# Attention and a max-out layer on one core: the linear layers on seven blocks of 512 tokens instead of eight of 448

## The chip, the core and the metric

The kernel runs on one core of one Trainium2 chip. A core has a matrix engine (TensorE, PE in the profile; its weight loads, LDWEIGHTS, stand in a row of their own, PEld), a vector engine (VectorE, DVE), a scalar engine (ScalarE, ACT), a general engine (GpSimd, POOL) and SyncE (SP), whose queue issues the DMA transfers here. Operands lie in on-chip memory (SBUF) of 128 partitions; matmuls write to PSUM banks of 512 float32 a partition. The metric is device time of one execution in microseconds.

## The reference, cut to what matters

```python
# q, k, v: (8, 12, 448, 64) float32
scores = scale * np.matmul(q, k.transpose(0, 1, 3, 2)) - np.log(S)      # S = 448, scale = 1/8
attn = 1.0 / (1.0 + np.exp(-scores))
attn_out = np.matmul(attn, v)
# x: 3584 tokens of 768 features; w1, w2, w3, w_out: 768 x 768
x = attn_out.transpose(0, 2, 1, 3).reshape(B * S, H * D)
h = np.maximum(np.maximum(x @ w1, x @ w2), x @ w3)
return (h @ w_out).astype(np.float32)
```

## The kernel before

**Attention.** 24 rounds, one for each group of four heads of a batch element. A round loads the next round's q and k (two tiles `qk`) and v through SyncE's queue (`load`), computes scores by TensorE (`scores`, `last_scores`, L330 and L342), their sigmoid on ScalarE (L312), and the weighted sums of v (`weigh`, `last_weigh`, L350 and L359). VectorE splits q/k into a high and a low part of the reduced-precision type float32r (`qk_split`, L321 and L322), so that three cheap products stand for one float32 product. `finish` copies a round's result from PSUM (L378) and stores it to the DRAM tensors `x_dram` (L379), features by tokens, in two halves of 384 features. Beside it each round decodes one piece of the weights (`decode`, L165 to L204), and GpSimd makes sums of weight blocks (`w_combine`, L141).

**Linear layers.** Two layers: three matrices w1, w2, w3 with the maximum over them, then w_out. Each matrix is cut in halves both ways, and a *pair* of token blocks makes the other factor two by two, so that seven products of sums of blocks stand for eight (`PRODUCTS`: name of the weight sum, name of the token sum, PSUM bank). A *visit* is one of four stages (three blocks of output features of layer one, then layer two) for one pair; it runs three outputs q, each with seven products of nine matmuls (three float32r terms for three slices of 128 features, `product`, L451). With 448 tokens a block there are four pairs and 16 visits.

**Token operands.** A pair's four blocks are loaded whole (`x_block`, L218), four differences made by GpSimd (`x_combine`, L229), then each of seven operands is split: `x_hi` on ScalarE (L260), `x_lo` on VectorE (L264), into tiles of their own (`xhi_*`, `xlo_*`). For the first pair the loads and differences run inside attention, rounds 9 to 20. The differences of layer one are stored to `t_dram` once (`t_store`, L242), and stages 1 and 2 load all seven operands from there and `x_dram` (`x_load_all`).

**What sets the order.** Every instruction is pinned to the order of the program text on its engine; SyncE's queue is in that order too, and a DMA whose data is not ready holds all behind it. In the linear layers, tables keyed by (visit, output, product) say after which product a split (`his`, `los`), a weight split (`ws`), a weight load (`w_loads`) or a decode is issued. `put` takes a product from PSUM (L521 to L529) and, at the end, stores it to `h_dram` or `outT` (L537).

Of the kernel before, what the change touches and what calls it, by code (L numbers as in the profile page):

```python
# [17 lines left out]
P = 128  # L18
D = 64

LEAST = 1.125 * 2.0**-15

# [12 lines left out]
    ("s4", "b22", 2),  # L35
)
# [3 lines left out]
def attention_then_maxout(  # L40
# [8 lines left out]

# [43 lines left out]
    t_dram = [dram.tile([P, 4, HALF, S], F32, name=f"t_dram{p}") for p in range(B // 2)]  # L93
# [6 lines left out]
    xs_p = pool(ctx, "xs", 1)  # L100
    m_p = pool(ctx, "m", 1)
    xo_p = [pool(ctx, "xo", 1)]
    ps_av = pool(ctx, "ps_av", 1, space=PSUM)


# [18 lines left out]
    def w_stage():  # L124
        return {name: ws_p.tile([P, HP], F32, name=f"ws_{name}") for name in BLOCKS}

# [6 lines left out]
        "s3": ("a11", "a21", ALU.subtract),  # L133
# [22 lines left out]
    def decoding(dec_p, todo, bufs, ahead, square_p):  # L156
# [11 lines left out]
        def decode(raw, out):  # L168
# [3 lines left out]
            square = square_p.tile([P, S], F32, name="c")[:, :HP]  # L172
# [35 lines left out]
    SUMS = {"t1": ("b12", "b11"), "t2": ("b22", "t1"), "t3": ("b22", "b12"), "t4": ("b21", "t2")}  # L208
    TOKENS = tuple(SUMS)

    def x_block(r, src, p, row, th, k=None):

        name = f"b{row + 1}{th + 1}"
        if name not in r:
            r[name] = xs_p.tile([P, HALF, S], F32, name=f"xs_{name}")
        ks = slice(0, HALF) if k is None else slice(k, k + 1)
        t = (2 * p + th) * S
        pin(nc.sync.dma_start(out=r[name][:, ks], in_=src[row][:, ks, t : t + S]))  # L218

    def x_combine(r, names=TOKENS, ks=range(HALF)):  # L220

        for name in names:
            if name not in r:
                r[name] = (
                    r["b12"] if name == "t3" else xs_p.tile([P, HALF, S], F32, name=f"xs_{name}")
                )
            in0, in1 = SUMS[name]
            for k in ks:
                pin(nc.gpsimd.tensor_tensor(  # L229
                    out=r[name][:, k], in0=r[in0][:, k], in1=r[in1][:, k], op=ALU.subtract  # L230
                ))

    def x_load(src, p):
        r = {}
        for row, th in ((0, 0), (0, 1), (1, 1), (1, 0)):
            x_block(r, src, p, row, th)
        x_combine(r)
        return r

    def t_store(r, p):  # L240
        for k, name in enumerate(TOKENS):
            pin(nc.sync.dma_start(out=t_dram[p][:, k], in_=r[name]))  # L242

    def x_load_all(p):
        r = {}
        for _, name, _ in PRODUCTS:
            if name in TOKENS:
                tile_name = "xs_b12" if name == "t3" else f"xs_{name}"
                r[name] = xs_p.tile([P, HALF, S], F32, name=tile_name)
                pin(nc.sync.dma_start(out=r[name], in_=t_dram[p][:, TOKENS.index(name)]))  # L250
            else:
                x_block(r, x_dram, p, int(name[1]) - 1, int(name[2]) - 1)
        return r

    FIRST = [x for _, x, _ in PRODUCTS[:1]]

    def x_hi(name, r):
        hi = xo_p[name not in FIRST].tile([P, HALF, S], F32R, name=f"xhi_{name}")
        lo = xo_p[name not in FIRST].tile([P, HALF, S], F32R, name=f"xlo_{name}")
        pin(nc.scalar.copy(out=hi, in_=r[name]))  # L260
        return name, r[name], hi, lo

    def x_lo(name, x, hi, lo):
        pin(nc.vector.tensor_tensor(out=lo, in0=x, in1=hi.bitcast(F32), op=ALU.subtract))  # L264
        x_ops[name] = hi, lo


    def attention(stack):


# [102 lines left out]
        def finish(n, pss, pool=m_p, names=("m11", "m12")):  # L373
            b, f = fours[n]
            for g, ps in enumerate(pss):
                k = 2 * f + g
                o = pool.tile([P, S], F32, name=names[g])
                pin(nc.vector.tensor_copy(out=o, in_=ps[:, :S]))  # L378
                pin(nc.sync.dma_start(  # L379
                    out=x_dram[k // HALF][:, k % HALF, b * S : (b + 1) * S], in_=o  # L380
                ))

# [9 lines left out]
        before, xs = None, {}  # L392
        terms = [(loads[0][0][0],) * 2]
        for n in range(len(fours) + 1):
# [10 lines left out]
            else:  # L405
                for name in FIRST:
                    x_lo(*x_hi(name, xs))
            if before:
# [6 lines left out]
                finish(n - 1, pss)  # L415
            last = last_scores(ts)
# [5 lines left out]
            part = n - 9  # L422
            if 0 <= part < 4 * HALF:
                k, block = divmod(part, 4)
                row, th = ((0, 1), (0, 0), (1, 1), (1, 0))[block]
                x_block(xs, x_dram, 0, row, th, k)
                x_combine(xs, ((), ("t1",), ("t2", "t3"), ("t4",))[block], (k,))
            if n == len(fours) - 1:
                t_store(xs, 0)
# [5 lines left out]
        return xs, lambda *to: finish(len(fours) - 1, pss, *to)  # L435

    with ExitStack() as stack:
        xs, finish = attention(stack)


    xo_p.append(pool(ctx, "xo2", 1, reuse_waits="tile"))
# [4 lines left out]
    def product(ps, w, x, first):  # L446
# [3 lines left out]
        for n, (wt, xt, k) in enumerate(terms):  # L450
            pin(nc.tensor.matmul(  # L451
                ps[:, :S], wt[:, k * P : (k + 1) * P], xt[:, k],
# [3 lines left out]


    pairs = list(range(B // 2))
    visits = [(st, p) for st in range(STAGES) for p in (pairs[::-1] if st == 1 else pairs)]
    done, LAST = len(visits), STAGES - 1  # L460

    his, los, ws, w_loads = {}, {}, {}, {}

    for n in range(1, done):
# [16 lines left out]
        if (st == LAST, p) != (st0 == LAST, p0):  # L483
            for k, (_, name, _) in enumerate(PRODUCTS):
                his[n - 1, 2, k] = name
            keys = [(n - 1, 2, k) for k in range(1, 5)] + [(n, 0, k) for k in (0, 2, 3)]
            for key, (_, name, _) in zip(keys, PRODUCTS):
                los[key] = name
    w_next, split = {}, {}

    decodes = [
        (n, *at)
        for n in range(len(pairs) - 1, 3 * len(pairs) - 1)
        for at in ((0, 6), (1, 3), (1, 6))
    ]
# [4 lines left out]
    x_first = xs  # L500
    for _, name, _ in PRODUCTS[1:4]:
        x_lo(*x_hi(name, xs))
    next(background)
    for k in (1, 2, 3):
        his[0, 0, k - 1] = los[0, 0, k] = PRODUCTS[k + 3][1]

    for n, (st, p) in enumerate(visits):
        nst, np_ = visits[n + 1] if (n, 2, 0) in his else (None, None)
        if nst in (1, 2):
            xs = x_load_all(np_)  # L510
        m = {}
        for q in range(3):
            ps, p1, u2, u3 = {}, None, None, None

            def put(name, y, add):

                y = y[:, :S]
                if st == LAST or q == 0:
                    m[name] = m_p.tile([P, S], F32, name=f"m{name}")
# [6 lines left out]
                else:  # L526
                    c = c_p.tile([P, S], F32, name="c")
                    pin(nc.vector.tensor_tensor(out=c, in0=y, in1=add, op=ALU.add))
                    pin(nc.vector.tensor_tensor(out=m[name], in0=c, in1=m[name], op=ALU.max))  # L529
                if st == LAST or q == 2:  # L530
                    half, t = int(name[0]) - 1, (2 * p + int(name[1]) - 1) * S
                    if st == LAST:
                        row = (q + 3 * half) * P
                        dst = outT[row : row + P, t : t + S]
                    else:
                        dst = h_dram[half][:, st, t : t + S]
                    pin(nc.sync.dma_start(out=dst, in_=m[name]))  # L537

            for k, (wname, xname, bank) in enumerate(PRODUCTS):
                here = n, q, k  # L540
                first = k < 4 or bank == 1
                if first:
                    ps[bank] = ps_y.tile(
                        [P, 512], F32, name=f"ps_y{bank}", bufs=2 if bank < 2 else 1
                    )
# [77 lines left out]
```

## Time and profile before

| | |
|---|---|
| time, median of 3 runs (lowest, highest) | 884.38 us (882.63, 886.62) |
| span of the profiled execution | 882.5 us |
| TensorE busy | 874.1 us (99%) |
| weight loads (PEld) | 696.1 us (79%) |
| VectorE | 621.3 us (70%) |
| ScalarE | 392.9 us (45%) |
| GpSimd | 183.2 us (21%) |
| moved by DMA | 161.87 MB, mean 183 GB/s |

A single run's time and the profiled execution's span are two measures: the span goes from the first to the last instruction of one execution, and that execution's own time is not among the three. Ends of matmuls are modelled in the profile, so a busy TensorE is not one at its peak; the starts are measured, and the step from one start to the next is what a matmul costs in a full stream.

### The profile page before, as it was taken

The numbers are of one execution on the slowest core, as the hardware profiler recorded it, in microseconds if no ns is written. First come the engines' busy times: TensorE is split into PE (matmuls) and PEld (weight loads), VectorE is DVE, ScalarE is ACT, GpSimd is POOL, SyncE is SP. The second block draws the span as 40 slices with busy tenths as digits, with TensorE's granted clock in tenths as the row PEclk, the third lists the DMA queues.
The fourth block names the chain that finished last, engine by engine and source line by source line (L and its number), as shares of the span: only waits on it lengthen the run. The fifth ranks groups of instructions, "written<-read, shape, count | busy, mean of one in ns | idle before, by whom it ended". The sixth has DMA issues, their size and how long they took to land. (4 is left out here: it accounts for less than half of the span.)

```text
span 882.5 us, 12993 instructions
## 1 busy us (share of the span) xinstructions
PE 874.1 (99%) x4866; PEld 696.1 (79%) x4866; DVE 621.3 (70%) x875; ACT 392.9 (45%) x499; POOL 183.2 (21%) x148
## 2 busy tenths in 40 slices
PE   8999999999999999999999999999999999999998
PEld 4544455444459999999999999999999998899997
DVE  3677568766866948678696888878778596736442
ACT  5777767776672413342353343235334253423320
POOL 0100022023102563502100020210001543760600
PEclk9999999999999999999999999999999999999999
DMA  6667666786647455414745642484563426162412
GB/s 225 208 227 240 226 236 224 243 279 228 214 158 275 174 217 165 174 50 141 292 159 207 241 147 70 148 298 170 182 263 114 150 77 222 65 209 94 169 72 83
DMA packets 74350, 161.87 MB, mean 183 GB/s; under 512 B 6960, under 2 KB 53808, under 8 KB 74288
## 3 DMA queue, kind: packets, MB, share of 16 engines
q1 hardware_dynamic: 74208, 160.82, 52.0%
q8 instruction: 38, 0.62, 0.3%
q10 hardware_dynamic: 80, 0.23, 0.1%
q14 instruction: 24, 0.20, 0.1%
HBM read 109.90 MB, written 51.12 MB: 182 GB/s over the span
## 5 line engine op out<-in xcount | busy, mean ns | idle before, releaser
L312 ACT ACTIVATE a<-ps_s,bias_s 128x896 f32<-128x896 f32 x168 | 156.4, 1007 | 78.6 <-PE ps_s L342 59.4
L451 PE MATMUL ps_y<-xhi_t,wlo_s 128*128 128x448 f32 x432 | 158.1, 366 | 0.1
L451 PE MATMUL ps_y<-xhi_t,whi_s 128*128 128x448 f32 x432 | 158.0, 366 | 0.0
L451 PE MATMUL ps_y<-xlo_t,whi_s 128*128 128x448 f32 x432 | 157.9, 366 | 0.0
L350 PE MATMUL ps_av<-a,v 128*64 128x448 f32 x576 | 118.6, 548 | 0.0
L451 PE MATMUL ps_y<-xhi_b,wlo_a 128*128 128x448 f32 x288 | 105.4, 366 | 0.0
L451 PE MATMUL ps_y<-xlo_b,whi_a 128*128 128x448 f32 x288 | 105.3, 366 | 0.0
L451 PE MATMUL ps_y<-xhi_b,whi_a 128*128 128x448 f32 x288 | 105.3, 366 | 0.0
L141 POOL TENSOR_TENSOR ws_s<-ws_a,ws_a 128x384 f32<-128x384 f32 x12 | 14.3, 1194 | 412.9 <-DMA ws_a<-w_dram 315.8
L549 ACT COPY p<-ps_y 128x448 f32<-128x448 f32 x48 | 25.5, 531 | 156.4 <-PE ps_y L451 156.4
L451 PEld LDWEIGHTS ps_y<-xhi_t,wlo_s 128*128 128x128 f32 x432 | 81.3, 188 | 6.8 <-ACT xhi_b L260 0.5
L451 PEld LDWEIGHTS ps_y<-xhi_t,whi_s 128*128 128x128 f32 x432 | 81.3, 188 | 6.3
L451 PEld LDWEIGHTS ps_y<-xlo_t,whi_s 128*128 128x128 f32 x432 | 81.3, 188 | 6.2
L350 PEld LDWEIGHTS ps_av<-a,v 128*64 128x64 f32 x576 | 37.2, 136 | 59.4 <-issue 57.9
L523 DVE TENSOR_TENSOR m<-ps_y,u 128x448 f32<-128x448 f32 x72 | 44.7, 621 | 55.9 <-PE ps_y L451 55.9
L229 POOL TENSOR_TENSOR xs_t<-xs_b,xs_t 128x448 f32<-128x448 f32 x48 | 64.2, 1363 | 37.0 <-DMA xs_b<-x_dram 36.0
L264 DVE TENSOR_TENSOR xlo_t<-xs_t,xhi_t 128x1344 fp32r<-128x1344 f32 x42 | 68.4, 1628 | 3.0 <-ACT xhi_t L260 3.0
L521 ACT COPY m<-ps_y 128x448 f32<-128x448 f32 x24 | 12.8, 533 | 125.8 <-PE ps_y L451 122.2
L552 DVE TENSOR_TENSOR u<-ps_y,p 128x448 f32<-128x448 f32 x48 | 29.9, 622 | 53.6 <-PE ps_y L451 52.5
L264 DVE TENSOR_TENSOR xlo_b<-xs_b,xhi_b 128x1344 fp32r<-128x1344 f32 x42 | 66.5, 1584 | 0.0
L260 ACT CAST xhi_t<-xs_t 128x1344 fp32r<-128x1344 f32 x42 | 55.5, 1322 | 17.7 <-PE ps_y L451 9.0
L175 ACT ACTIVATE c<-wraw 128x384 f32<-128x384 f32 x48 | 27.0, 563 | 75.4 <-DVE m L529 44.9
(68 smaller groups left out, 1636.1 us busy)
## 6 DMA issues: line engine op xcount, KB each, us to landing
qk<-qk SPq DMA_DIRECT2D x47, 448.0 KB, 5.6
xs_b<-x_dram SPq DMA_DIRECT2D x30, 672.0 KB, 7.0
wraw<-w SPq DMA_DIRECT2D x36, 384.0 KB, 4.9
xs_t<-t_dram SPq DMA_DIRECT2D x18, 672.0 KB, 8.0
v<-v SPq DMA_DIRECT2D x24, 448.0 KB, 3.8
h_dram<-m SPq DMA_DIRECT2D x48, 224.0 KB, 1.9
xs_b<-h_dram SPq DMA_DIRECT2D x16, 672.0 KB, 6.5
outT<-m SPq DMA_DIRECT2D x48, 224.0 KB, 1.9
```

The lines of the kernel that those rows point to most:

```text
L141: pin(nc.gpsimd.tensor_tensor(out=r[name], in0=r[in0], in1=r[in1], op=op))
L175: pin(nc.scalar.activation(out=square, in_=high.bitcast(F32), func=AF.Square))
L229: pin(nc.gpsimd.tensor_tensor(out=r[name][:, k], in0=r[in0][:, k], in1=r[in1][:, k], op=ALU.subtract))
L260: pin(nc.scalar.copy(out=hi, in_=r[name]))
L264: pin(nc.vector.tensor_tensor(out=lo, in0=x, in1=hi.bitcast(F32), op=ALU.subtract))
L312: pin(nc.scalar.activation(out=a, in_=ps[:, :, :S], func=AF.Sigmoid, bias=bias_s, scale=scale))
L350: pin(nc.tensor.matmul(ps[e * D : (e + 1) * D, :S], vt[:, (g * C + c) * 2 + e], a[:, e], start=c == 0, stop=False,))
L451: pin(nc.tensor.matmul(ps[:, :S], wt[:, k * P : (k + 1) * P], xt[:, k], start=first and n == 0, stop=n == len(terms) - 1, skip_group_check ...
L521: pin(nc.scalar.copy(out=m[name], in_=y))
L523: pin(nc.vector.tensor_tensor(out=m[name], in0=y, in1=add, op=ALU.add))
L549: pin(nc.scalar.copy(out=p1, in_=ps[0][:, :S]))
L552: pin(nc.vector.tensor_tensor(out=u2, in0=ps[1][:, :S], in1=p1, op=ALU.add))
```

## The change

The tokens of the linear layers are taken as seven blocks of `BLK` = 512, across the borders of batch elements: three pairs of blocks, and one single block. A pair still takes seven products per output. The single block takes four (`SINGLE`): with b1 and b2 its upper and lower features, `a11 b1`, `s3 b1`, `a22 b2` and `a12 b2`, with `s3` now `a21 - a11`; the differences `t1` and `t3` change their form accordingly. A stage visits pair 0, the single block, pair 1, pair 2 (stage 1 in the order 2, single, 1, 0).

Token differences of both layers now go through DRAM. `sums` loads the two rows of blocks for 2 x 256 tokens of one slice of 128 features into one tile `sum`, GpSimd makes four differences of 256 tokens in place, and a store puts all four to `t_dram`. It is a generator of three steps (load, differences, store); one step is made at each `add_up`: three times in an attention round, from round 10 on, and twice in each output of the linear layers. A pair takes six such pieces for each of the two layers.

Operands rotate through ten equal tiles `xl` (`XL`): `x_fetch` loads the next operand in the list `todo_x` as soon as a tile is spare, which is after the last product that reads it; six of the tiles are used in attention already, one load a round from round 16 on. `x_lo` writes the low part over the loaded tile; only the high parts have tiles of their own, and the single block's share those of `t2` and `t1`.

```diff
+SINGLE = (
+    ("a11", "b1", 0),
+    ("s3", "b1", 1),
+    ("a22", "b2", 1),
+    ("a12", "b2", 0),
+)
...
-        "s3": ("a11", "a21", ALU.subtract),
+        "s3": ("a21", "a11", ALU.subtract),
...
+    XL, EARLY = 10, 6
+    SUMS = (((0, 0), (0, 1), (0, 0)), ((0, 1), (0, 1), (1, 1)),
+            ((1, 1), (1, 1), (0, 0)), ((1, 0), (1, 0), (1, 1)))
+    WIDE = BLK // 2
+
+    def sums(src, layer, p, k):
+        for c in range(2):
+            r = sum_p.tile([P, 2, 2, WIDE], F32, name="sum")
+            for row in range(2):
+                tokens = src[row][:, k, 2 * p * BLK : 2 * (p + 1) * BLK]
+                tokens = tokens.rearrange("p (h c n) -> p h c n", h=2, c=2)
+                pin(nc.sync.dma_start(out=r[:, row], in_=tokens[:, :, c]))
+            yield
+            for out, in0, in1 in SUMS:
                 pin(nc.gpsimd.tensor_tensor(
-                    out=r[name][:, k], in0=r[in0][:, k], in1=r[in1][:, k], op=ALU.subtract
+                    out=r[:, out[0], out[1]], in0=r[:, in0[0], in0[1]],
+                    in1=r[:, in1[0], in1[1]], op=ALU.subtract,
                 ))
+            yield
+            dst = t_dram[layer, p][:, :, k, c * WIDE : (c + 1) * WIDE]
+            pin(nc.sync.dma_start(out=dst, in_=r.rearrange("p a b n -> p (a b) n")))
...
+    def x_fetch(most=XL):
+        while todo_x and spare and spare[0] < most:
+            n, st, p, name = todo_x[0]
+            layer = int(st == STAGES - 1)
+            ready = ((layer, p) in summed) if p < PAIRS else whole[layer]
+            if not ready:
+                return
...
+            pin(nc.sync.dma_start(out=t.bitcast(F32), in_=src))
+            loaded[n, name] = i, t
...
+    def x_lo(n, name):
+        _, x, hi = loaded[n, name]
+        pin(nc.vector.tensor_tensor(
+            out=x, in0=x.bitcast(F32), in1=hi.bitcast(F32), op=ALU.subtract
+        ))
+        x_ops[n, name] = hi, x
...
+            add_up(n)
             last = last_scores(ts)
             second = [scores(terms, c) for c in range(C)]
             if n + 1 < len(fours):
                 terms = qk_split(loads[n + 1][0][0])
             decode()
...
+            if n >= 16:
+                x_fetch(min(EARLY, n - 15))
+            add_up(n)
             pss = [ps_av.tile([P, 512], F32, name=f"ps_av{g}") for g in range(2)]
             for c in range(C):
                 weigh(pss[0], vt, 0, c, first[c])
+            add_up(n)
...
             pin(nc.tensor.matmul(
-                ps[:, :S], wt[:, k * P : (k + 1) * P], xt[:, k],
+                ps, wt[:, k * P : (k + 1) * P], xt[:, k],
...
+                if leaving and q == 2 and xname not in [x for _, x, _ in steps[n][k + 1 :]]:
+                    x_free(base[n], xname)
+                    x_fetch()
...
+                if k in ((1, 3) if single else (2, 5)):
+                    add_up()
+                    x_fetch()
```

How SyncE's queue changes in attention: these are its DMAs of round 17, from the stores of the round before's result to the loads of the next round. Before (`m` is the copied result, `wraw` an encoded weight piece, `xs_b` a block of the first pair):

```order
L379 DMA x_dram_64<-m_2131 128x448
L379 DMA x_dram_65<-m_2134 128x448
L165 DMA wraw<-w 128x384
L218 DMA xs_b_1249<-x_dram_64 128x448
L302 DMA qk<-qk 128x896 x2
L307 DMA v<-v 128x896
```

And now:

```order
L370 DMA x_dram_64<-m_2171 128x448
L370 DMA x_dram_65<-m_2174 128x448
L206 DMA sum<-x_dram_64 128x2x256
L206 DMA sum<-x_dram_65 128x2x256
L148 DMA wraw<-w 128x384
L240 DMA xl_2230<-t_dram_68 128x1536
L215 DMA t_dram_69<-sum 512x1x256
L293 DMA qk<-qk 128x896 x2
L298 DMA v<-v 128x896
```

The q/k and v loads of the next round now stand behind a store of the sums that are made in the same round, and behind an operand load.

On GpSimd, rounds 17 to 20 before (`ws` are weight sums, which wait for the decode of their round, and `xs_t`, `xs_b` the first pair's token differences):

```order
L141 TENSOR_TENSOR ws_s_2185<-ws_a_2064,ws_a_2065 128x384
L141 TENSOR_TENSOR ws_s_2297<-ws_s_2185,ws_a_2062 128x384
L141 TENSOR_TENSOR ws_a_2064<-ws_a_2062,ws_a_2064 128x384
L229 TENSOR_TENSOR xs_t_1365<-xs_b_1249,xs_b_1363 128x448
L141 TENSOR_TENSOR ws_s_2411<-ws_a_2063,ws_s_2297 128x384
```

And now, rounds 17 to 19:

```order
L124 TENSOR_TENSOR ws_s_2228<-ws_a_2099,ws_a_2100 128x384
L209 TENSOR_TENSOR sum<-sum 128x256 x4
L124 TENSOR_TENSOR ws_s_2349<-ws_s_2228,ws_a_2097 128x384
L124 TENSOR_TENSOR ws_a_2099<-ws_a_2099,ws_a_2097 128x384
L209 TENSOR_TENSOR sum<-sum 128x256 x4
L124 TENSOR_TENSOR ws_s_2471<-ws_a_2098,ws_s_2349 128x384
```

In these rounds a weight sum stands ahead of the four token sums on whose store the queue waits.

Between visits, SyncE's queue before loaded a pair's seven operands in one piece, here for a visit of stage 2:

```order
L218 DMA xs_b_4947<-x_dram_64 128x3x448
L250 DMA xs_t_4949<-t_dram_68 128x1344
L250 DMA xs_b_4951<-t_dram_68 128x1344
L250 DMA xs_t_4953<-t_dram_68 128x1344
L218 DMA xs_b_4955<-x_dram_65 128x3x448
L250 DMA xs_t_4957<-t_dram_68 128x1344
L218 DMA xs_b_4959<-x_dram_65 128x3x448
```

And now, between pairs 1 and 2 of stage 0, where three of the seven were loaded earlier (`m` here are outputs of the visit that ends, stored to `h_dram`):

```order
L240 DMA xl_3760<-t_dram_70 128x1536
L240 DMA xl_3776<-x_dram_65 128x3x512
L240 DMA xl_3793<-t_dram_70 128x1536
L557 DMA h_dram_67<-m_3587 128x512
L240 DMA xl_3816<-x_dram_65 128x3x512
L557 DMA h_dram_66<-m_3598 128x512
L240 DMA xl_3830<-x_dram_64 128x3x512
L557 DMA h_dram_67<-m_3610 128x512
```

The loads are issued one by one, as each product of the last output frees its tile, with the stores of the outputs among them.

More of the change, by code (lines that the diff above doesn't have):

```diff
@@ L19 @@
 D = 64
+BLK = 512
 LEAST = 1.125 * 2.0**-15
@@ L91, in attention_then_maxout @@
     h_dram = [dram.tile([P, HALF, T], F32, name=f"h_dram{r}") for r in range(2)]
-    t_dram = [dram.tile([P, 4, HALF, S], F32, name=f"t_dram{p}") for p in range(B // 2)]
+    PAIRS = T // (2 * BLK)
+    t_dram = {
+        (layer, p): dram.tile([P, 4, HALF, BLK], F32, name=f"t_dram{layer}{p}")
+        for layer in range(2)
+        for p in range(PAIRS)
+    }
     def pool(stack, name, bufs, **kw):
@@ L205, in decoding @@
                 yield
[L208 to L228, printed above, removed]
+    XL, EARLY = 10, 6
+    SOURCE = {"b11": (0, 0), "b21": (1, 0), "b22": (1, 1), "b1": (0, 0), "b2": (1, 0)}
+    T_AT = {"t1": 0, "t3": 1, "t4": 2, "t2": 3}
+    SLOT = {"b1": "t2", "b2": "t1"}
@@ new lines, in attention_then_maxout, with x_hi @@
+    whole = [False, False]
+    def x_hi(n, name):
+        slot = SLOT.get(name, name)
+        hi = xh_p[slot != NAMES[0]].tile([P, HALF, BLK], F32R, name=f"xhi_{slot}")
+        pin(nc.scalar.copy(out=hi, in_=loaded[n, name][1].bitcast(F32)))
+        loaded[n, name] += (hi,)
+    def x_lo(n, name):
[4 more added lines that the diff above has]
+        x_ops[n, name] = hi, x
@@ L268, in attention, with x_free @@
+    def x_free(n, name):
+        spare.append(loaded.pop((n, name))[0])
     def attention(stack):
@@ L381, in finish, with add_up @@
                 ))
+        def add_up(n):
+            while n > x_ready[adding[0]] and next(adders[adding[0]], False) is False:
+                adding[0] += 1
         load(0)
@@ L405, in attention @@
             else:
-                for name in FIRST:
-                    x_lo(*x_hi(name, xs))
+                x_hi(0, NAMES[0])
+                x_lo(0, NAMES[0])
             if before:
@@ L507, in attention_then_maxout, with add_up @@
+    adders = adders[adding[0] : PAIRS]
+    def add_up():
+        while adders and next(adders[0], False) is False:
+            adders.pop(0)
+    base = []
     for n, (st, p) in enumerate(visits):
-        nst, np_ = visits[n + 1] if (n, 2, 0) in his else (None, None)
-        if nst in (1, 2):
-            xs = x_load_all(np_)
+        fresh = n == 0 or (st == LAST, p) != (visits[n - 1][0] == LAST, visits[n - 1][1])
+        base.append(n if fresh else base[-1])
+    for n, (st, p) in enumerate(visits):
```

175 lines of the change are left out of this document (91 added, 84 removed).

## The prediction

> **What bounds the kernel now.** I read the page first, then the busy times by stage, then the steps between matmuls, and last the attention loop on the engines that feed it.
>
> ```profile
> span 882.5 us, 12993 instructions
> ...
> PE   8999999999999999999999999999999999999998
> PEld 4544455444459999999999999999999998899997
> ```
>
> ```profile
> 0.00:262.00 262.00, 259.74 (x1843) 127.96 (x1844) 179.93 (x282) 181.55 (x220) 32.57 (x28) 1.00 0.66 224
> 262.00:880.00 618.00, 614.40 (x3024) 568.17 (x3024) 441.39 (x594) 211.35 (x279) 150.64 (x120) 1.00 0.47 167
> ```
>
> TensorE (PE) is busy in every slice, at a granted clock of 1.00 in both windows (columns of a window: length, then PE, weight loads, VectorE, ScalarE, GpSimd busy with counts, clock, DMA share, GB/s). The first 262 us are attention, the rest the linear layers: 3024 matmuls in 618 us, with VectorE at 441 and ScalarE at 211. Nothing but TensorE fills the linear stage, so its cost is the number of matmuls times the step from one to the next, plus waits.
>
> ```profile
> 300.00:700.00 400.00, 400.00 (x1976) 371.26 (x1975) 1.00 0.51 181
> ```
>
> ```profile
> L451 PEld LDWEIGHTS ps_y<-xhi_t,wlo_s x432: 186/188/189, 263.6 to 872.3; 128*128 128x128 f32 x144
> L451 PE MATMUL ps_y<-xhi_t,wlo_s x432: 361/366/442, 263.8 to 872.5; 128*128 128x448 f32 x144
> ```
>
> ```profile
> 772.71 106.05 PE ps_y L451 x521
> ```
>
> The first of these rows counts the linear matmuls that touch a stretch without waits, the next two are the minimum, median and maximum of a group of weight loads and of its matmuls in ns, and the last is the end of the chain that finished last. A matmul lasts 0.366, so 1.8 of the 1976 are counted for the edges, and the step is 400.00/1974.2 = 0.2026 us. 3024 steps make 612.7. The stage runs from 261.9 to the end of the chain's last matmul piece, 772.71 + 106.05 = 878.8, that is 616.9; about 4 us are waits.
>
> **The matmuls after.** Seven blocks need 4 stages x 3 outputs x (3 x 7 + 4) x 9 = 2700 matmuls of 512 columns in place of 4 x 3 x 4 x 7 x 9 = 3024 of 448: 10.7% fewer instructions, 2.0% more columns. Everything hangs on what the 0.2026 consists of. The weight load (0.188) plus some 0.015 of handing over would give the same figure, and then 64 more columns would nearly be free. So I looked for a matmul whose load came late.
>
> ```profile
> 85.95 0.37 PE L330 MATMUL ps_s<-hi,lo 64*128 64x448 f32 x2
> 86.15 0.43 PE L330 MATMUL ps_s<-hi 64*128 64x448 f32 x2
> 86.42 0.37 PE L330 MATMUL ps_s<-lo,hi 64*128 64x448 f32 x2
> ```
>
> ```profile
> 86.11 0.19 PEld L330 LDWEIGHTS ps_s<-hi 64*128 64x128 f32 x2 [0.17 <-ACT a L312]
> 86.22 0.19 PEld L330 LDWEIGHTS ps_s<-lo,hi 64*128 64x128 f32 x2
> ```
>
> These are score matmuls of the same operand kind and width (two at a time, in two halves of the rows). At 86.11 a load waited for ScalarE and began 0.16 after the matmul ahead (85.95). Its own matmul still took its turn at 86.15, 0.20 after the one ahead, and was only recorded 0.06 longer than the usual 0.37; the next load followed 0.11 after the late one. So weights are ready about 0.11 after their load begins, whether a matmul streams or not, and the 0.20 turn is there without them. A load that begins on time has 0.09 to spare. I read the 0.2026 as the time that the columns themselves occupy.
>
> ```profile
> 150.87 0.14 PEld L350 LDWEIGHTS ps_av<-a,v 128*64 128x64 f32 x2 [0.23 <-issue]
> ...
> 152.00 0.14 PEld L350 LDWEIGHTS ps_av<-a,v 128*64 128x64 f32 x2 [0.23 <-issue]
> ```
>
> No row has 512 columns, so I bound the step. In proportion it is 0.2026 x 512/448 = 0.2315. If a fixed part stays fixed, only the 64 columns are added. These f32 pairs step three times in 1.13, 0.377 each; taken as two passes over 448 columns (an estimate) that is 0.42 ns a column, so 0.2026 + 0.027 = 0.2295. I take 0.231, near the row scaled in proportion, because nothing in the rows shows a fixed part. Then 2700 x 0.231 = 623.7, against 612.7: **11.0 us more** (7.0 at 0.2295, 12.4 at 0.2315).
>
> The Trainium skill, TensorE: Matmul & The Clock Gate, section Back-to-back issue gap, gives an isolated gap of N/2.4 + 2.5 ns. That is 189 ns at 448 columns, and the trace's 202.6 disagrees; taken at 512 it would be 215.8 ns, 2700 of them 582.7 us, 30 less than now.
>
> VectorE, ScalarE: the same elementwise work in pieces a seventh larger on 2% more columns; the windows leave both over a quarter of the linear stage idle, so I put it at nothing beside TensorE. If that cover were gone, 2% of 441 is 9 us on VectorE. GpSimd makes 144 sums of 256 elements in place of 96 of 448, less in total.
>
> **The token sums in attention.** This is the wait that is added. The timeline shows one round of the loop, from one copy of results (L378) to the next (start, duration, engine, line); behind it stand the issues' median time to landing and the spread of two groups on GpSimd.
>
> ```profile
> 165.84 0.88 SPq L302 DMA_DIRECT2D qk<-qk  x2
> ...
> 168.88 1.16 DVE L378 COPY m<-ps_av 128x448 f32<-128x448 f32 x2 [1.43 <-PE ps_av L359]
> ...
> 169.54 1.07 SPq L379 DMA_DIRECT2D x_dram<-m  x2
> ...
> 169.96 0.62 DVE L321 CAST hi<-qk 128x896 fp32r<-128x896 f32 x1
> ...
> 170.61 1.09 DVE L322 TENSOR_TENSOR lo<-qk,hi 128x896 fp32r<-128x896 f32 x1
> ...
> 174.04 0.47 PE L330 MATMUL ps_s<-hi 64*128 64x448 f32 x2
> ...
> 174.96 0.56 DVE L186 SCALAR_TENSOR_TENSOR wb<-c,wb 128x384 f32<-128x384 f32 x1
> ...
> 176.45 0.88 SPq L302 DMA_DIRECT2D qk<-qk  x2
> ...
> 179.48 1.16 DVE L378 COPY m<-ps_av 128x448 f32<-128x448 f32 x2 [2.30 <-PE ps_av L359]
> ```
>
> ```profile
> xs_b<-x_dram SPq DMA_DIRECT2D x12, 224.0 KB, 4.7
> ```
>
> ```profile
> L229 POOL TENSOR_TENSOR xs_t<-xs_b,xs_t x48: 1136/1160/2505, 134.5 to 831.4; 128x448 f32<-128x448 f32 x48
> ```
>
> ```profile
> L141 POOL TENSOR_TENSOR ws_s<-ws_s,ws_a x12: 1008/1211/2222, 38.0 to 740.8; 128x384 f32<-128x384 f32 x12
> ```
>
> Take F = 168.88, the copy. SyncE's queue sends the next q/k tiles at F + 7.6, held until then by the store of decoded weights. Tiles sent at 165.84 are split at 169.96 without a wait; the split ends at 171.70 and TensorE uses it at 174.04, so 2.3 us are free, and q/k could leave at F + 9.9. After the change the store of the sums stands ahead of them and waits for GpSimd. The sum loads go behind the two result stores (F + 1.7) and land 4.7 later, the second at about F + 6.9. Four sums follow; 448 elements take at best 1.136 and 384 take 1.008, 2.0 ns an element, so 256 take 0.75 and four 3.0: F + 9.9. With 0.4 to issue the store, q/k leave at F + 10.3, and 0.1 MB more is ahead of them: 0.6 us late. It happens in 12 rounds (10 to 21): 7 us. In four of them (11, 17, 18, 19) weight sums stand ahead on GpSimd; they wait for the decode (174.96 + 0.56 = F + 6.6) and take 1.2 each, two in round 18, so the token sums begin 1.0 (three times) and 2.2 later: 5 more. Behind the held store wait the q/k and v tiles, for them the VectorE split, and for that TensorE's scores. Less some overlap, since sums that are late in one round also delay the next round's loads, which have slack of their own, I take **10 us**. Low end 0: the row's load is shorter where the queue is empty and the 2.3 us absorb all. High end 20: each sum at the slow durations above (up to 2.5).
>
> The Trainium skill, SBUF — State Buffer, section Who interferes with whom, says that a VectorE instruction with two SBUF inputs and a GpSimd instruction that reads SBUF shut each other out; the spread from 1.136 to 2.505 agrees, and its price would be inside the high end.
>
> ```profile
> 9.00:12.00 3.00, 3.00 (x24) 1.26 (x21) 1.80 (x3) 2.62 (x4) 0.00 (x0) 1.00 1.03 413
> ```
>
> ```profile
> xs_t<-t_dram SPq DMA_DIRECT2D x18, 672.0 KB, 8.0
> ```
>
> **The linear operands.** A pair now reads 7 x 0.79 MB in every stage, from tiles that come free one product at a time: 0.79 MB per 9 x 0.231 = 2.08 us is 378 GB/s, under the 413 seen. The first is wanted four products (8.3 us) after its slot is freed, and such loads landed in 8.0. So I leave the waits at 4 us, bounds 0 to 14. What hides these loads is the matmul stream itself; without it each of ten fresh pair visits would pay its lateness.
>
> Sum against the profiled execution: 882.5 + 11.0 + 10 = 903.5. Its span lies 1.9 under the median of the runs (884.4), so **905**.
>
> **Rivals.**
>
> *Weight load as the floor* (ends faster). If the turn is load plus hand-over, 512 columns cost their f32 rate, 512 x 0.42 = 0.215. 2700 x 0.215 = 580.5, 32 less than now; with the 10 of attention 882.5 - 32.2 + 10 + 1.9 = 862 (850 to 872). For it: 0.188 + 0.015 fits exactly, and LDWEIGHTS is the fullest row of the linear stage. Against it: the late load. The gap rule of the Trainium skill quoted above (TensorE: Matmul & The Clock Gate, Back-to-back issue gap) would give this rival's step. The rival decides the sign if the 512-column step is under 0.227, where 2700 steps equal 612.7. Chance 0.18.
>
> *Sums hidden*: the loads land early enough, attention stays at 262: 882.5 + 11 + 1.9 = 895 (886 to 898). For it: the 2.3 us of slack and a DMA share of only 0.66. Against: the queue's order. Chance 0.18.
>
> *Starved linear layers*: operand loads land 2 us late in ten visits: 905 + 20 = 925. For it: 378 GB/s in bursts behind other traffic. Against: early tiles are three slots ahead. Chance 0.05.
>
> *Forecast*: slower stream and a late attention loop, 905 (897 to 917), chance 0.57. The remaining 0.02 is no change through cancelling pieces.
>
> The range 884 to 920 leaves out the faster rival and most of the starved one, 0.20 to 0.22 together; the likeliest case alone spans 897 to 917. A measurement of this kernel can tell about 0.5% (4.4 us) from no change. Faster by more: 0.18. Within: 0.05, the low edge of the hidden-sums case and the remainder. Slower by more: 0.77.
>
> **What would show it.** Right: linear matmuls step by 0.2295 to 0.2315 with a full clock, and the linear stage takes about 628; in attention the rounds from 10 on last over 11 us instead of 10.6 and VectorE's cast of q/k shows idle time ended by the qk DMA, while SyncE's longest waits name GpSimd's sums. Wrong: a step near 0.215 refutes my reading of the late load, and with it the sign; rounds of 10.6 us refute the second term; idle TensorE time ended by operand loads or their splits would be the third rival.

## The result and the profile after

The changed kernel takes 939.88 us (median of 4 runs, 936.22 to 941.18) against 883.76 for the kernel before (four runs, 882.63 to 886.62): a ratio of 1.0622, 95% interval 1.0593 to 1.0651. It is slower, as forecast, but by 56 us instead of 20, and the time lies above the range.

First the page's span, TensorE's row of 40 slices and its granted clock:

```profile
span 939.4 us, 12333 instructions
...
PE   9999988789687989999999999999999999999998
...
PEclk9999999898899989999999999999999999999999
```

The full row of nines of before has gaps from the sixth to the fifteenth slice, that is in attention and just behind it, and the clock falls below nine there too. The linear layers behind them look as before. Next the windows of three stages and, last, a stretch without waits (length, PE, weight loads, VectorE, ScalarE, GpSimd busy with counts, clock, DMA share, GB/s):

```profile
0.00:314.60 314.60, 276.77 (x1843) 135.06 (x1843) 187.58 (x281) 182.88 (x221) 63.28 (x68) 0.95 0.71 236
314.60:338.00 23.40, 18.39 (x70) 13.72 (x67) 15.62 (x14) 7.85 (x7) 10.95 (x8) 0.85 0.48 158
338.00:936.00 598.00, 597.75 (x2636) 494.24 (x2634) 398.37 (x502) 191.50 (x252) 122.30 (x120) 1.00 0.59 202
400.00:800.00 400.00, 400.00 (x1766) 331.12 (x1765) 301.44 (x394) 135.85 (x190) 100.71 (x100) 1.00 0.63 215
```

Attention lasts until 314.6; its 1843 matmuls took 262 before. In the stretch from 400 to 800, 1766 matmuls less 1.7 for the edges (0.389 over the step) are 1764.3, a step of 0.2267; 2700 steps are 612.0, against 612.7 for the 3024 narrower ones. From the first linear matmul (314.6) to the end of the last (935.7) it is 621.2 against 616.9, so waits grew from 4.2 to 9.2. The whole difference of the two spans, 56.9, is then **52.7 in attention, 5.0 in waits at the start of the linear layers, and -0.7 for all the wider matmuls**.

The timeline shows one turn of SyncE's queue in attention, with what VectorE and GpSimd do between (start, duration, engine, line, idle before and what ended it):

```profile
202.26 1.16 DVE L369 COPY m<-ps_av 128x448 f32<-128x448 f32 x2 [1.07 <-PE ps_av L350]
...
203.42 0.52 SPq L215 DMA_DIRECT2D t_dram<-sum  x1
...
204.03 1.57 SPq L293 DMA_DIRECT2D qk<-qk  x2
...
205.69 0.42 SPq L298 DMA_DIRECT2D v<-v  x1
...
206.16 1.18 SPq L370 DMA_DIRECT2D x_dram<-m  x2
...
207.44 1.61 SPq L206 DMA_DIRECT2D sum<-x_dram  x2
208.87 0.63 DVE L312 CAST hi<-qk 128x896 fp32r<-128x896 f32 x1 [5.46 <-DMA qk<-qk]
...
213.83 3.60 POOL L209 TENSOR_TENSOR sum<-sum 128x256 f32<-128x256 f32 x4 [10.44 <-DMA sum<-x_dram]
...
217.46 0.53 SPq L215 DMA_DIRECT2D t_dram<-sum  x1
217.51 1.16 DVE L369 COPY m<-ps_av 128x448 f32<-128x448 f32 x2 [3.08 <-PE ps_av L350]
```

Read it as a circle. The store at 203.42 had to wait for GpSimd; at once behind it go q/k, v and the result stores, and only then the next chunk's sum loads (207.44). They land 6.4 later, the four sums take 3.6, and only then can the store at 217.46 go. One turn is 14.0 us, and TensorE's round, 10.6 before, must follow it. VectorE's cast stood 5.46 idle until q/k landed. The first store and the thirteenth, the last that SyncE issues in attention, are twelve turns apart:

```profile
129.17 0.59 SPq L215 DMA_DIRECT2D t_dram<-sum  x1
```

```profile
308.44 0.52 SPq L215 DMA_DIRECT2D t_dram<-sum  x1
```

That is 14.9 a turn on average, 4.4 over a round of 10.6, and twelve times that is 52 of the 52.7. In every one of these turns SyncE issues everything from the store to the next sum loads with no gap above 0.45; what it waits for last, ahead of the next store, is GpSimd. TensorE's granted clock falls to 0.50 in seven stretches of attention, 31 us in all, and its matmuls are busy 276.77 there instead of 259.74. Since the queue waits for no matmul between a store and the next sum loads, I read the clock as a consequence of the late q/k and not as a cause of the turn; no run tests it apart. Over the whole kernel, in the waits of the engines and of SyncE's queue (total, times, longest):

```profile
DVE hi L312 <- DMA qk<-qk: 70.1, 14, 7.8
```

```profile
SPq L215 <- POOL sum L209: 80.3, 23, 7.5
...
SPq L206 <- DMA t_dram<-sum: 47.3, 13, 8.3
```

The stall at the start of the linear layers is of the same kind. The chain that ended last, and then VectorE's timeline in the same stretch and a window of the matmuls just behind the stall:

```profile
315.79 1.36 POOL sum L209
...
317.22 2.15 POOL sum L209
...
323.87 0.52 SPq L215
...
324.49 5.67 DMA xl<-x_dram
...
330.18 1.48 ACT xhi_b L248
...
331.68 1.77 DVE xl L253
```

```profile
314.80 6.19 DVE L253 TENSOR_TENSOR xl<-xl,xhi_t 128x1536 fp32r<-128x1536 f32 x3
```

```profile
334.20:337.60 3.40, 3.40 (x10) 2.66 (x9) 1.19 (x3) 0.00 (x0) 2.09 (x3) 0.50 0.71 216
```

A store of sums holds the load of the seventh operand, and of its four sums the first takes 1.36 and the others 2.15 to 2.19, instead of 0.75, while VectorE makes the operands' low parts. TensorE waits 6.1 in three pieces from 327.5, and the matmuls behind them run at a granted clock of 0.50, ten in 3.4 us, which adds 2 more. This agrees with two pages of the Trainium skill: SBUF — State Buffer, Who interferes with whom (the rule the prediction cited) and TensorE: Matmul & The Clock Gate, Back-to-back issue gap, which gives N/1.2 for a cold array: 426.7 ns at 512 columns, where these starts stand 426 to 427 apart.

### The profile page after: what moved, and what is told of

Same layout as the page of the kernel before. It is cut to its first block, busy times and chain, and to the rows that moved or that the text cites. A ratio compares the mean times of both kernels' runs of the same rounds, so it can differ in the third digit from the quotient of the medians.

```text
span 939.4 us, 12333 instructions
## 1 busy us (share of the span) xinstructions
PE 892.9 (95%) x4542; PEld 643.0 (68%) x4542; DVE 602.1 (64%) x795; ACT 382.2 (41%) x479; POOL 196.5 (21%) x196
## 2 busy tenths in 40 slices
DMA packets 106284, 199.00 MB, mean 212 GB/s; under 512 B 8176, under 2 KB 60400, under 8 KB 106224
## 4 chain that ended last, share of the span: by engine, by line
PE 84%; DMA 9%; DVE 2%; POOL 2%; issue 1%; SPq 1%; ACT 1%; POOLq 0%; ACTq 0%; DVEq 0%
PE ps_y L460 64%; PE ps_s L321 8%; PE ps_av L341 8%; DMA qk<-qk 6%; DMA sum<-x_dram 2%; POOL sum L209 2%; PE ps_av L350 2%; PE ps_s L333 2%; DVE lo L313 1%; DVE hi L312 1%; DMA xl<-x_dram 1%; DMA t_dram<-sum 0%; ACT a L303 0%; SPq L215 0%; POOL ws_a L124 0%
## 5 line engine op out<-in xcount | busy, mean ns | idle before, releaser
L209 POOL TENSOR_TENSOR sum<-sum 128x256 f32<-128x256 f32 x144 | 138.5, 962 | 386.4 <-DMA sum<-h_dram 228.8
L460 PE MATMUL ps_y<-xl,whi_s 128*128 128x512 f32 x468 | 183.1, 391 | 1.0 <-DVE xl L253 1.0
L460 PE MATMUL ps_y<-xl,whi_a 128*128 128x512 f32 x432 | 168.7, 390 | 0.0
L460 PE MATMUL ps_y<-xhi_t,whi_s 128*128 128x512 f32 x360 | 140.1, 389 | 0.0
L460 PE MATMUL ps_y<-xhi_t,wlo_s 128*128 128x512 f32 x360 | 140.0, 389 | 0.0
L460 PEld LDWEIGHTS ps_y<-xl,whi_s 128*128 128x128 f32 x468 | 88.2, 189 | 20.3 <-DVE xl L253 2.0
L253 DVE TENSOR_TENSOR xl<-xl,xhi_t 128x1536 fp32r<-128x1536 f32 x48 | 87.4, 1824 | 2.3 <-ACT xhi_t L248 2.3
L460 PE MATMUL ps_y<-xhi_b,wlo_a 128*128 128x512 f32 x216 | 84.4, 391 | 0.0
L460 PE MATMUL ps_y<-xhi_b,whi_a 128*128 128x512 f32 x216 | 84.1, 389 | 0.0
L460 PE MATMUL ps_y<-xhi_t,wlo_a 128*128 128x512 f32 x216 | 84.0, 389 | 0.0
```

Of the source, the lines that this page charges most:

```text
L209: pin(nc.gpsimd.tensor_tensor(out=r[:, out[0], out[1]], in0=r[:, in0[0], in0[1]], in1=r[:, in1[0], in1[1]], op=ALU.subtract,))
L253: pin(nc.vector.tensor_tensor(out=x, in0=x.bitcast(F32), in1=hi.bitcast(F32), op=ALU.subtract))
L460: pin(nc.tensor.matmul(ps, wt[:, k * P : (k + 1) * P], xt[:, k], start=first and n == 0, stop=n == len(terms) - 1, skip_group_check=not first,
```

## The experiments

The theory from this reading: **a closed turn on SyncE's queue**. The store that waits for GpSimd holds the q/k loads, and the late q/k loads stand ahead of the next chunk's sum loads, so each chunk's lateness is part of the next one's. Rivals: the bytes (199.00 MB are moved in place of 161.87) make q/k land late; the one `sum` buffer; GpSimd and VectorE in each other's way. A chunk is one tile of sums; attention has 14 of the 18 of layer one.

### Without the subtractions

```diff
-            for out, in0, in1 in SUMS:
+            for out, in0, in1 in SUMS if layer else ():
```

> Leaves out the four subtractions of each chunk of attention's token sums (36 of the 72 of the first 18 chunks stand in attention's own rounds); the two loads and the store of each chunk stay, in their places on SyncE's queue, with the same bytes. Closed-loop theory: in the changed kernel a round lasts as long as one turn of SyncE's queue, 14.1 us from one store of sums to the next (203.42 to 217.46): 5 of issues, 5 to 6 of landing, 3.6 of sums. Without the sums the turn is 10.4 to 10.5, under the 10.6 of a round of before; attention ends by 262 to 268 and the whole takes 882 to 892. Traffic theory (more bytes make the q/k tiles land late): the bytes are the same, so attention ends at about 310 and the whole takes 930 to 940. Single-buffer theory (the next chunk's loads wait until the store has landed): the store leaves 3.6 earlier too, so this run cannot tell it from the closed loop.

Measured: 895.5 us; the first linear matmul starts at 277.4, so 37 of the 52.7 went and 15.5 stayed, more than expected. Its timeline on SyncE's queue shows why:

```profile
183.55 0.53 SPq L215 DMA_DIRECT2D t_dram<-sum  x1
...
187.45 1.18 SPq L206 DMA_DIRECT2D sum<-x_dram  x2
...
194.72 0.52 SPq L215 DMA_DIRECT2D t_dram<-sum  x1
```

This turn is 11.2, not 10.4, and the average from the first store to the thirteenth is 11.8: the loads took over 7 to land, and the store still waits for them, so the circle still misses the 10.6 of a round. The traffic theory's 930 to 940 is refuted, all bytes being there. (The run leaves out all 72 subtractions of layer one, of which 56, the 14 chunks in attention, bear on this, not 36.)

### Without any sums in attention

```diff
-    summed = set()
+    summed = {(0, p) for p in range(T // (2 * BLK))}
...
-            if name in T_AT:
+            if name in T_AT and layer:
...
-    adders = [sum_all(x_dram, 0, p) for p in range(PAIRS)] + [None]
+    adders = [iter(()) for p in range(PAIRS)] + [None]
```

> Leaves out the whole of attention's token sums (loads, subtractions, stores); the operands of the first three linear stages that would be sums are read from the unsummed tokens, with as many bytes, and the early operand loads in attention's last rounds stay. Closed-loop theory: attention ends at 262 to 264 as before, the stall of 6 us at the start of the linear layers goes, 2700 steps of 0.2267 are 612, so 877 to 882 in all. If the early operand loads (six of 0.79 MB in rounds 16 to 21) also hold the q/k tiles, attention ends at 267 or later and the whole takes over 886.

Measured: 880.2 us, first linear matmul at 261.8. The first window is that of before but for GpSimd's part:

```profile
0.00:262.00 262.00, 259.77 (x1843) 127.92 (x1843) 175.43 (x282) 182.13 (x221) 17.08 (x16) 1.00 0.68 231
```

The early operand loads cost attention nothing. All of the 52.7 belongs to the sums' loads, subtractions and stores.

### Two buffers, same order

```diff
-    XL, EARLY = 10, 6
+    XL, EARLY = 10, 5
...
+            own = sum2[0] if c == 1 and layer == 0 and p < 2 else sum_p
-            r = sum_p.tile([P, 2, 2, WIDE], F32, name="sum")
+            r = own.tile([P, 2, 2, WIDE], F32, name="sum")
```

> A second buffer for the chunks of the first two pairs, taken from one early operand tile (five instead of six); every place on the queues stays. Single-buffer theory: the next chunk's loads no longer wait for the store's landing (47 us of SyncE's waits in the changed kernel), rounds fall to about 11 us and the whole to 895 or less. Closed-loop theory: those waits lie where SyncE has time, the loads stand behind the held store and the late q/k loads either way, so rounds stay at 13 to 15 and the whole at 928 to 945.

Measured: 942.9 us, first linear matmul at 314.4. SyncE still waits for the sums nearly as long as with one buffer (its queue's waits):

```profile
SPq L216 <- POOL sum L210: 74.2, 22, 7.0
```

The buffer alone is not the cause.

### Two buffers, and the store a round later

Beside the edits of the run before:

```diff
+            for c in range(2):
+                steps = sums(src, layer, p, k, c)
+                next(steps)
+                if held:
+                    next(held)
+                yield
+                next(steps)
+                held = steps
+                yield
+        if held:
+            next(held)
...
                 weigh(pss[0], vt, 0, c, first[c])
-            add_up(n)
```

> The two buffers, and each chunk's store one round later, behind the next chunk's loads (which stand behind the q/k, v and result transfers); two calls a round instead of three, the third pair's chunks with one buffer. Same sums, same bytes. Closed-loop theory: no q/k load stands behind a store that still waits for GpSimd, so rounds are 10.6 to 10.8 us, attention ends at 262 to 268, no operand load is held at the start of the linear layers, and the whole takes 877 to 888. Traffic theory: 925 to 940, since nothing of the traffic is gone. Theory of the shared access of VectorE and GpSimd: the same sums slow the same splits, 925 to 940.

Measured: 885.7 us in three rounds (ratio to before 1.0003, interval 0.9971 to 1.0035), first linear matmul at 261.9. The window of attention:

```profile
0.00:262.00 262.00, 258.19 (x1843) 126.89 (x1843) 188.66 (x281) 181.79 (x221) 64.15 (x68) 1.00 0.81 280
```

The same sums, GpSimd as busy (64.15 for 63.28), the same bytes in a shorter time (280 GB/s for 236), and attention takes 262. Traffic and disturbed engines are out as causes of the lateness; where the store stands, together with room for a second chunk, decides. The linear layers have stalls of 1.6 and 0.6 us here, so this order gives back the loss and no more.

### One buffer, the store behind the q/k loads

```diff
                 load(n + 1)
+                add_up(n - 1)
...
                 weigh(pss[0], vt, 0, c, first[c])
-            add_up(n)
```

> One buffer as in the changed kernel; only the place of each chunk's store on SyncE's queue differs: behind the next round's q/k and v loads, ahead of the result stores and of the next chunk's loads. If the place of the store ahead of the q/k loads were the whole cause, rounds are 10.6 to 11 and the whole takes 880 to 892. Closed-loop theory: the loop finds another way round, since the next chunk's loads stand right behind the store and wait for its landing as well (0.5 of issue, 3.5 of landing, 0.9 of issue, 5 to 6 of landing, 3.6 of sums: 13.5 to 14.5), and SyncE stands still in that wait with the following q/k loads behind it, so rounds stay at 12.5 to 14.5 and the whole at 915 to 940.

Measured: 900.7 us, first linear matmul at 282.6: between the two expectations. The circle does find its other way, at the length expected, but only in part of the rounds: the first five turns, to 186.35, take 11.4 on average. Its queue in a round where it does:

```profile
196.53 0.54 SPq L215 DMA_DIRECT2D t_dram<-sum  x1
197.12 1.35 SPq L370 DMA_DIRECT2D x_dram<-m  x2
203.57 0.88 SPq L206 DMA_DIRECT2D sum<-x_dram  x2
...
210.26 0.52 SPq L215 DMA_DIRECT2D t_dram<-sum  x1
```

The loads into the same buffer go 7.0 after the store, with SyncE standing still from 198.5 on; 13.7 a turn. Of the 52.7, 32 go with the place of the store alone.

### The store on GpSimd's own queue, with two buffers and with one

The version with two buffers has the edits of "Two buffers, same order" beside this one.

```diff
-            pin(nc.sync.dma_start(out=dst, in_=r.rearrange("p a b n -> p (a b) n")))
+            queue = nc.sync if layer else nc.gpsimd
+            pin(queue.dma_start(out=dst, in_=r.rearrange("p a b n -> p (a b) n")))
```

> Two buffers, every place as in the changed kernel, but each chunk's store of attention's sums is issued from GpSimd's own queue, behind the sums it carries. Same loads, sums, bytes. Closed-loop theory: SyncE holds nothing that waits for GpSimd; a chunk's loads have two rounds for loads, sums and store, so rounds are 10.6 to 11, attention ends at 262 to 270 and the whole takes 877 to 892. If it is the sums themselves (engines that disturb each other) or their bytes, 925 to 942.

> The kernel of store_gpsimd again, now timed in five rounds: two buffers, attention's stores of sums on GpSimd's queue. One run of it took 882.1 beside 885.4 of the kernel before. The changed blocks bring 2700 steps of 0.2267 for 3024 of 0.2026, 0.7 us less, and fewer stalls in the linear layers than before (0.8 for 4); attention about 1 us more. Expected: 880 to 884, a ratio to before of 0.995 to 1.000, that is no change or a gain of half a per cent at most.

> As store_gpsimd, but with one buffer and six early operands as in the changed kernel. If only SyncE's wait for GpSimd matters, one buffer is enough: attention ends at 262 to 270 and the whole takes 880 to 890. If the chunk's own turn counts too, the next loads wait on SyncE for the store's landing: 0.9 of issue, 5 to 6 of landing, 3.6 of sums, 6 for the store from GpSimd's queue, 15.5 to 16.5 a chunk against 10.6 a round, with the q/k loads behind that wait in every second or third round: attention ends at 285 to 315, the whole takes 905 to 935.

With two buffers: 882.1 us in one run, and in five rounds **881.9 (879.79 to 883.8) against 885.66 for before, ratio 0.9949, interval 0.9922 to 0.9975**. Beside the run with two buffers and the old order nothing else was moved: with the wait for GpSimd on GpSimd's own queue, attention's cost is gone. Of the versions that compute all sums it is the only one that beats both kernels, by 0.5% against all 17 runs of before and by 0.3% against the 12 of them that lie below 887 (median 884.6; the other five took 891 to 892). Its profile:

```profile
0.00:262.00 262.00, 259.24 (x1842) 127.62 (x1842) 186.00 (x281) 181.79 (x221) 70.62 (x81) 1.00 0.81 281
262.00:878.00 616.00, 613.36 (x2704) 506.36 (x2700) 414.49 (x515) 200.04 (x259) 133.01 (x133) 1.00 0.60 204
```

From the first linear matmul (262.0) to the end of the last (875.4) it is 613.3: 612.0 of steps and 1.3 of waits, where the kernel before has 612.7 and 4.2. So the 3.0 us between the profiled spans (879.5 and 882.5) are mostly waits, not matmuls.

With one buffer: 914.1 us, first linear matmul at 294.2. SyncE then waits in the loads for the store to land:

```profile
SPq L206 <- DMA t_dram<-sum: 119.3, 20, 9.9
```

So the four cases of queue and buffers are 939.9 and 942.9 (SyncE, one and two), 914.1 and 881.9 (GpSimd, one and two). Neither half is enough: the wait for GpSimd must not stand ahead of the q/k loads (on GpSimd's queue it does not, nor a round later on SyncE's, in the run with two buffers that took 885.7), and the chunk's own turn (loads, sums, store, landing) needs two rounds.

### A chunk in every second round

```diff
-            while n > x_ready[adding[0]] and next(adders[adding[0]], False) is False:
+            while n % 2 == 0 and n > x_ready[adding[0]] and next(adders[adding[0]], False) is False:
...
-                if k in ((1, 3) if single else (2, 5)):
+                if n < 2 or k in ((1, 3) if single else (2, 5)):
                     add_up()
+                if k in ((1, 3) if single else (2, 5)):
                     x_fetch()
```

> The changed kernel with a chunk of sums in every second round of attention only (rounds 10, 12, ... 22: 7 chunks in place of 14); the rest follow in the first two visits of the linear layers, at every product, so the linear stage has other stalls and only attention's end is read here. It ends at 262 without sums and at 314.6 with a chunk in every round, 52.6 for 14 chunks, 3.8 a chunk. If each chunk costs by itself and nothing feeds back, 7 chunks cost 26 and attention ends at 286 to 292. If a late q/k load delays the next chunk's loads behind it and that is part of the price, a round without a chunk breaks the loop, a chunk costs 2.5 or less, and attention ends at 270 to 280.

Measured: 968.1 us, with starved operands in the linear layers; attention ends at 295.5, beyond both expectations. One interval explains that, in the chain that ended last:

```profile
265.10 12.90 DMA qk<-qk
```

Six operand loads of 0.79 MB stood right ahead of it (from 261.3), all released at once as the first pair's sums were ready only then; q/k, usually 5 to 6, took 12.9. So the end of attention can't be compared, but the intervals before it can. The table has the time from one copy of results to the next less the 10.58 of the run without sums, in us, from the first chunk's store on:

| interval | 1 | 2 | 3 | 4 | 5 | 6 | 7 | 8 | 9 | 10 | 11 | 12 |
|---|---|---|---|---|---|---|---|---|---|---|---|---|
| a chunk in each | 7.4 | 4.6 | 1.6 | 7.2 | 1.7 | 4.6 | 3.6 | 2.8 | 8.2 | 3.8 | 5.0 | 1.8 |
| in 1, 3, 5, 7, 9, 11 | 6.0 | 1.2 | 1.6 | 0.3 | 1.9 | 0.0 | 2.1 | 0.0 | 6.5 | 1.2 | 2.1 | (12.4) |

Alone, a chunk costs 1.6 to 2.1, and next to nothing in the round after; where two sums of weight blocks stand ahead on GpSimd (1 and 9), 6.0 to 6.5 and 1.2 after. Ten chunks at 1.9 and two at 7.5 would be 34; the changed kernel has 52 in these intervals. The remaining 18 is what a chunk in each round adds to chunks alone. It is a difference of totals; single intervals prove less, since the granted clock is at 0.50 for 3.4 or 6.8 us in intervals 1, 2, 4, 6, 7, 9 and 11 of the first row (the seven stretches above), and in 1, 9 and 12 of the second, where it may be part of the 6.0 and 6.5.

### The step by columns

```diff
+    for cols in (512, 448, 384, 320, 256, 192, 128, 64):
+        for rep in range(2):
+            acc = ps_y.tile([P, BLK], F32, name="ps_y0", bufs=2)
+            for n in range(18):
+                wt = w_ops[2][("a11", "a22", "a12", "s4")[n % 4]][n // 4 % 2]
+                k = n % HALF
+                pin(nc.tensor.matmul(
+                    acc[:, :cols], wt[:, k * P : (k + 1) * P], probe_x[n % 2][:, k, :cols],
+                    start=n == 0, stop=n == 17, skip_group_check=True,
+                ))
```

> The changed kernel with 8 x 36 matmuls added behind the last product, with 512, 448, 384, 320, 256, 192, 128 and 64 columns, the weights changing every time as in the linear layers; their results are not used. Steps from matmul to matmul: if the columns set the step with a fixed part, the line through 448 (0.2027) and 512 (0.2267) gives 0.179 at 384, 0.155 at 320, 0.131 at 256, 0.083 at 128. If the weight load is the floor, the step stops falling at 0.19 to 0.20, that is from 400 columns down. If the weights are ready 0.11 after their load begins and nothing else holds them, it stops falling near 0.11, at 200 columns.

> The run of widths with other columns: 496, 480, 464, 456, 448, 440, 432, 416. There the steps at 512, 384, 320 and 256 columns lay on 13.3 ns + 0.4167 ns a column (226.7, 173.6, 146.7, 120.0), and 448 took 202.7 where that line gives 200.0. If only 448 is off, the others lie on it: 220.0, 213.3, 206.7, 203.3, 196.7, 193.3, 186.7. If the line has a step of 2.7 ns somewhere between 384 and 512 or the neighbours of 448 are off as well, they lie 2 to 3 above it.

Their own times (982.3 and 988.1) say nothing, the matmuls being additional. TensorE's timeline of the first run, second and last matmul of 448, 256 and 192 columns (36 of each):

```profile
942.66 0.37 PE L621 MATMUL ps_y<-xl,whi_a 128*128 128x448 f32 x1
...
949.55 0.36 PE L621 MATMUL ps_y<-xl,whi_a 128*128 128x448 f32 x1
...
961.41 0.28 PE L621 MATMUL ps_y<-xl,whi_a 128*128 128x256 f32 x1
...
965.48 0.28 PE L621 MATMUL ps_y<-xl,whi_a 128*128 128x256 f32 x1
...
965.69 0.28 PE L621 MATMUL ps_y<-xl,whi_a 128*128 128x192 f32 x1
...
969.49 0.27 PE L621 MATMUL ps_y<-xl,whi_a 128*128 128x192 f32 x1
```

34 steps each: 0.2026, 0.1197 and 0.1118. The table has the mean distance of starts in ns for each width, without the first five, the spread of single steps, and the line 13.3 + columns x 0.4167, which was fitted to 256 and 512:

| columns | step | single steps | line |
|---|---|---|---|
| 512 | 226.7 | 226 to 227 | 226.7 |
| 496 | 220.0 | 220 | 220.0 |
| 480 | 216.7 | 212 to 221 | 213.3 |
| 464 | 210.0 | 205 to 215 | 206.7 |
| 456 | 208.7 | 200 to 217 | 203.3 |
| 448 | 202.7, second run 206.7 | 199 to 207, second run 206 to 207 | 200.0 |
| 440 | 200.0 | 198 to 201 | 196.7 |
| 432 | 196.1 | 189 to 203 | 193.3 |
| 416 | 188.2 | 183 to 191 | 186.7 |
| 384 | 173.3 | 173 to 174 | 173.3 |
| 320 | 146.7 | 146 to 147 | 146.7 |
| 256 | 120.0 | 120 | 120.0 |
| 192 | 111.7 | 110 to 114 | 93.3 |
| 128 | 111.6 | 110 to 115 | 66.7 |
| 64, to 975.4 us | 111.5 | 111 to 112 | 40.0 |

Columns set the step, with a fixed 13 ns; there is a floor, but at 0.112, from 192 columns down. That it is the weight load fits the load that followed 0.11 after the late one in the prediction, but no run here keeps the weights unchanged. At 64 columns the granted clock fell to 0.50 at 975.5 us, in the midst of a stream without waits, and the rest stepped by 213. The widths from 416 to 480 are off the line, most of them uneven from step to step, and 448 lies 2.7 to 6.7 above it. The expectation of the first run drew its line through 448 and so gave 178.7 for 384. Why these widths are uneven was not found.

## Why the prediction was wrong, step by step

**What bounds the kernel before**: right. TensorE's steps were the linear stage before and after; with the sums out of the way, nothing but 1 to 3 us stands beside them.

**The matmuls after, +11.0**: wrong; it is -0.7, below the stated lower bound of 7.0. Two readings in it held. The weight load does not set the step at these widths, and the 0.11 read from one late load is close to the floor that the narrow matmuls show (0.112). A column costs 0.42 ns (the line's slope). The failing step is "in proportion", and the lower bound shared its fault: both start from 0.2026, which I took for what 448 columns cost anywhere. 2.7 ns of it are particular to that width, and 13 are fixed ("nothing in the rows shows a fixed part"). The line gives 0.2267 at 512, within 0.0003 of the point from which the prediction said the sign turns. So 3024 steps of before lost 2.7 ns each, 8 us in all. The 2.0% more columns now cost 11.5, and 324 fixed parts fewer save 4.3, so the two sides nearly cancel. The isolated gap of the Trainium skill (TensorE: Matmul & The Clock Gate, Back-to-back issue gap) has the right slope, 1/2.4 ns a column, but 215.8 at 512 is 10.9 short of the 226.7 here.

**The token sums in attention, +10**: the mechanism and its place were right (the store ahead of q/k, held by GpSimd; casts idle until q/k land; long rounds from the first chunk on), the size was wrong: 52.7. This is the term that failed, at three places:

- A chunk alone was put at 0.6 and costs 1.9. The sum loads, taken at 4.7 from loads of 224 KB, have 256 KB each and landed in 6.4 in the turn shown, and four sums took 3.6 instead of 3.0. The "0.1 MB more" ahead of q/k is too little: a round's sum loads and store are 0.52 MB each, where before one block load of 0.23 MB stood. The 12 rounds are 14 (10 to 23).
- The weight sums ahead were put at 5 together, with one round in which two of them stand ahead. There are two such rounds (the other is round 10, the first), and in the run with every second round they cost 7.5 each with the round behind, 1.9 of it the chunk itself.
- "Less some overlap, since sums that are late in one round also delay the next round's loads, which have slack of their own". That sentence should have added, not taken off. The loads' start, the copy plus 1.7, was that of an undisturbed round; in the turn shown they go 5.2 after the copy, behind the late store and q/k. One queue holds store, q/k and loads, so there is no slack of their own: 18 of the 52, by the table's account.

The stated upper end, 20, came from slower sums, and its own figures give more: at 2.5 for 448 elements, 256 take 1.4 in proportion and four 5.7 instead of 3.0, in 12 rounds 33 on top of the 12. Slow sums were not what happened (median 0.74), and no bound was put on the turn as a whole: from store to store it was never added up, though every piece of it stood in the prediction.

**Waits of the linear layers, 4 (0 to 14)**: 9.2, within the bounds. Not the ten late visits of the starved rival, but one store of sums ahead of one load, its sums slow beside VectorE's work, and the clock behind it. The runs that free the queue have 1 to 3 us.

**VectorE and ScalarE at nothing**: right; in the window from 262 to 878 of the version with the store on GpSimd's queue VectorE is busy 414 and TensorE still 613 of 616.

**Rivals**: the weight load as the floor, no (512 columns step by 0.2267, not 0.215, the floor of narrow matmuls is 0.112, and LDWEIGHTS was not the fullest row of the linear stage: 568.17 beside TensorE's 614.40); the sums hidden, no, though two orders hide them fully; starved layers, no. What the range lacked was a case in which attention's loop is bound by the queue instead of TensorE.

## What to carry to other kernels

When a step that waits is put into an in-order queue, follow the queue once around: from the waiting instruction through everything issued behind it to what that instruction waits for next time. If the sum (here 14.0) exceeds the round (10.6), the loop runs at that pace, and no single lateness tells it. Give such a step the queue of the engine it waits for, or a place a round later, and buffers for as many rounds as its turn takes; either alone left 20 us or more of the loss. And when a matmul's width changes, measure the step at both widths before scaling one.

## What the runs showed of the hardware unexpectedly

Steps of these fp32r matmuls are even to a nanosecond at 256, 320, 384, 496 and 512 columns and spread over 3 to 17 ns at most widths from 416 to 480; 448 took an uneven 202.7 in one program and an even 206.7 in another. In the stream of ever narrower matmuls, without waits, the granted clock dropped from 1.00 to 0.50 in the midst of those of 64 columns, and their step went from 111.5 to 213 ns. Behind a burst of six operand loads of 0.79 MB the q/k tile landed in 12.9 us instead of 5 to 6, while one such load a round cost nothing.
